# Where the MLP's pieces stand in ScalarE's order: top-k attention and a leaky-ReLU MLP on one core

## The chip, the cores and the metric

The kernel runs on one core of a Trainium2 chip. The metric is the device time of one execution in microseconds (us). The kernel before took 1473.86 us in the median of 4 runs (1472.53 to 1476.35). In what follows PE is TensorE (matmuls), DVE VectorE, ACT ScalarE, POOL GpSimd and SP the engine that issues the DMAs.

## What is computed

Attention with 8 batches, 8 heads, 576 positions and head dimension 64, in which each query keeps its 32 largest scores; its output, as 4608 rows of 512, goes through a two-layer MLP with a leaky ReLU. All is in 32-bit floats.

```python
scores = scale * np.matmul(q, k.transpose(0, 1, 3, 2))
kth = np.partition(scores, -32, axis=-1)[..., -32:-31]
scores = np.where(scores >= kth, scores, -1e9)
attn = np.exp(scores - scores.max(-1, keepdims=True))
attn = attn / (attn.sum(-1, keepdims=True) + 1e-9)
x = np.matmul(attn, v).transpose(0, 2, 1, 3).reshape(4608, 512)
h = x @ w_in                                  # 512 x 2048
out = np.maximum(0.01 * h, h) @ w_out         # 2048 x 512
```

## The kernel before

**Units.** The attention is cut into 144 units. A unit is 128 query rows against 576 keys for two heads: either 128 queries of one pair of heads, or the last 64 queries of two pairs. A unit passes through a pipeline over several steps of the main loop (lines 536 to 589), one unit entering per step, so that step s works on four generations at once:

- `scores` (line 203) of units s+2 and s+3, every second step: matmuls into PSUM tiles `wide` and `narrow`, and four ScalarE copies to `s_sb` (line 227). `wide` has two buffers, shared with the values and with the transposes on TensorE; `narrow` has one.
- `top_k` (line 243) of unit s on VectorE: two elementwise operations, four rounds of max and match-replace, in four slots (`slot()`).
- `mask` (line 262) of unit s-1 on GpSimd, then `exponents` (line 271) of its two heads on ScalarE, which leave sums in `z`, and `sums` (line 275), which gives `ze`.
- of unit s-2: `reciprocals` on VectorE (`rz`, line 281), `normalize` for two heads (line 284), then `transpose` (line 286): two ScalarE copies split the 32-bit words into 16-bit halves (line 293), each half is written to DRAM by a DMA on SP's queue (line 294), and a DMA transpose brings them back as `wT` (line 296). Four units near the start (14, 15, 23 and 31) are transposed on TensorE (line 306) and copied by ScalarE (line 312).
- `weigh_values` (line 326): matmuls of `wT` with the values, for two units at a time; `keep_values` (line 340) copies the result to `x`. For units up to 13 this happens early in a step (place MIDDLE), later at its end (END); line 447 says in which step: for an odd unit n from 14 on, n+3, or n+2 for three hurried ones.

**The MLP.** It works on chunks of tokens: two of 128 and 17 of 256. `mlp` (line 377) is a generator; between its `yield`s it issues a few matmuls, and each `yield` gives a cost in columns. First layer: `ph` (line 389; 512 columns for two matmuls of 256), and after each pair of feature blocks a Prelu on ScalarE (line 395) that empties the PSUM buffer. Second layer: `pz` (line 401; 1024 for two matmuls of 512), and after 16 feature blocks a ScalarE copy (line 410) and an output DMA on SP. The first two chunks are handled otherwise (line 351): `ph` with x as weights (line 357), Prelu (line 362), and transposes `pt` of the result on TensorE (line 373; cost 256) with a ScalarE copy (line 374). `ph`, `pz` and `pt` share one pool of two PSUM buffers.

**The planner.** `mlp_steps(budget)` (line 423) issues a piece: it adds the budget to an account and runs the generator until the account is used up; a cost that overdraws it is paid off by the next pieces, which may then issue nothing. There are 7 pieces per step. The budget is 500 as long as at most two chunks have become ready, later the backlog spread evenly over the pieces up to the next chunk (line 472).

**What sets the order.** Every engine works through its own instructions in the order in which the loop issues them. TensorE's order is that of MLP pieces, values, scores and the transposes on TensorE; ScalarE's is that of normalizations, exponents, splits, the copies and the Prelus of the pieces. A change of the loop's order changes both, and a wait in either holds up all that stands behind it on that engine.

In a step of the kernel before, ScalarE meets: normalization; pieces 1 and 2; exponents of the first head; both splits; pieces 3, 4 and 5; exponents of the second head and `sums`; copies of values and scores; pieces 6 and 7. In the first 20 steps the normalization mostly stands behind piece 1.

## Time and profile before

| | |
|---|---|
| median of 4 runs | 1473.86 us |
| the profiled execution | 1472.53 us |
| its span, first to last instruction | 1470.6 us |
| mean clock granted to TensorE | 0.98 |
| weights rounded, up to about | 64 us |
| first MLP matmul at | 132.9 us |
| last instruction of VectorE's top-k, about | 1384 us |
| DMA transpose, issue to landing (median of 140) | 4.5 us |

The span is a little shorter than the execution, and the profiled execution is the fastest of the four runs; sums made from the trace are sums within it. An engine's busy share is a mean over stages with different bounds. Busy time, the rows of a timeline (start in us, duration in us, engine, line, operation, output<-inputs, and in brackets the idle time before and what ended it) and the lists of waits are shown with the prediction.

### The profile page before, as it was taken

To read this page: it belongs to the slowest core of one execution; us is meant where nothing else is said; L and a number is where in the kernel's file an instruction comes from. 1 tells how busy PE (TensorE), PEld (TensorE's weight loads), DVE (VectorE), ACT (ScalarE), POOL (GpSimd) and SP (SyncE) were. 2 spreads that over 40 slices of the span, in tenths; PEclk is the share of its full clock that TensorE was granted. 3 is DMA by queue.
4 is the path that set the end of the run, shared out by engine and by line. 5 is a ranking of instruction groups with operands and counts; after the bars stand their busy time and mean duration, and the time that the engine had idled before them with its cause. 6 is when DMAs were issued, how large, how long until landed. Compare 5 with 4: busy or idle time off the path is not lost.

```text
span 1470.6 us, 24096 instructions
## 1 busy us (share of the span) xinstructions
PE 1395.5 (95%) x8068; PEld 928.5 (63%) x8068; DVE 1322.6 (90%) x3400; ACT 1095.8 (75%) x1979; POOL 1098.0 (75%) x743
## 2 busy tenths in 40 slices
PE   7716989999999999999999999999999999999999
PEld 2304547676766666666666666766676767676674
DVE  6999999999999999999999999999999999999600
ACT  8657877877787777777777777787877787877720
POOL 3288877888788888788888888888888888788700
PEclk9957999999999999999999999999999999999999
DMA  9725442654367554666557545565457555554510
GB/s 348 283 75 134 138 112 89 173 168 137 105 171 216 131 144 130 184 173 153 135 166 199 151 128 145 159 199 144 128 166 207 144 134 135 164 137 134 145 47 14
DMA packets 388795, 222.29 MB, mean 151 GB/s; under 512 B 333888, under 2 KB 333888, under 8 KB 386624
## 3 DMA queue, kind: packets, MB, share of 16 engines
q1 hardware_dynamic: 388672, 220.77, 52.9%
q8 instruction: 63, 1.03, 0.3%
q14 instruction: 60, 0.49, 0.1%
HBM read 46.14 MB, written 92.01 MB: 94 GB/s over the span
## 4 chain that ended last, share of the span: by engine, by line
PE 86%; DVE 11%; DMA 1%; issue 1%; ACT 1%; POOL 0%; DVEq 0%; ACTq 0%
PE pz L401 33%; PE ph L389 32%; PE wide L333 11%; PE wide L220 6%; DVE tops L255 4%; PE narrow L220 3%; DVE pairs L258 3%; DVE pairs L250 1%; DMA raw<-in_weights_dram 1%; DVE w_in L155 1%; DVE scale L152 1%; DMA wT<-apart 0%; DVE w_out L155 0%; DVE scale L129 0%; DVE top L138 0%
## 5 line engine op out<-in xcount | busy, mean ns | idle before, releaser
L268 POOL TENSOR_SCALAR pen<-s_sb,tops 128x576 f32<-128x576 f32 x288 | 638.3, 2216 | 208.0 <-DVE tops L255 119.0
L255 DVE MAX8 tops<-pairs 128x8 f32<-128x288 f32 (+1 forms) x1152 | 637.8, 594 | 0.0
L401 PE MATMUL pz<-w_out,gT 128*128 128x512 f32 x1152 | 510.7, 598 | 4.9 <-ACT scale L362 4.9
L389 PE MATMUL ph<-x,w_in 128*128 128x256 f32 x2176 | 481.1, 381 | 0.0
L258 DVE MATCH_REPLACE8 pairs<-tops,pairs 128x288 f32<-128x288 f32 (+1 forms) x864 | 461.5, 541 | 0.0
L389 PEld LDWEIGHTS ph<-x,w_in 128*128 128x128 f32 x2176 | 410.7, 190 | 77.1 <-issue 22.9
L269 POOL TENSOR_TENSOR s_sb<-s_sb,pen 128x576 f32<-128x576 f32 x288 | 407.4, 1415 | 24.0
L401 PEld LDWEIGHTS pz<-w_out,gT 128*128 128x128 f32 x1152 | 215.6, 190 | 269.7 <-issue 263.5
L293 ACT COPY split<-s_sb 128x1152 uint16<-128x1152 uint16 x280 | 307.1, 1146 | 0.0
L284 ACT ACTIVATE s_sb<-s_sb,rz 128x576 f32<-128x576 f32 x288 | 207.1, 769 | 42.3 <-DVE rz L281 42.3
L272 ACT ACTIVATE s_sb<-s_sb,nbias 128x576 f32<-128x576 f32 x288 | 221.4, 769 | 12.5 <-POOL s_sb L269 12.5
L250 DVE TENSOR_TENSOR pairs<-s_sb 128x576 f32<-128x576 f32 x288 | 213.6, 780 | 9.9
L333 PEld LDWEIGHTS wide<-wT,vt 128*64 128x64 f32 x3200 | 161.7, 139 | 65.7 <-ACT s_sb L227 27.2
L333 PE MATMUL wide<-wT,vt 128*64 128x128 f32 (+1 forms) x3200 | 178.8, 268 | 23.5 <-ACT s_sb L227 21.8
L395 ACT ACTIVATE gT<-ph 128x512 f32<-128x512 f32 x136 | 80.8, 594 | 80.0 <-PE ph L389 80.0
L347 ACT COPY x<-wide 128x128 f32<-128x128 f32 (+1 forms) x160 | 32.1, 260 | 127.6 <-PE wide L333 127.5
L227 ACT COPY s_sb<-wide 128x704 f32<-128x704 f32 x142 | 107.1, 754 | 25.4 <-PE wide L220 25.3
L220 PE MATMUL wide<-kt,qt 64*128 64x352 f32 (+1 forms) x392 | 75.7, 499 | 26.6 <-ACT s_sb L227 23.6
L227 ACT COPY s_sb<-narrow 128x448 f32<-128x448 f32 x142 | 68.7, 536 | 1.1 <-PE narrow L220 0.5
L410 ACT COPY o_sb<-pz 128x512 f32<-128x512 f32 x36 | 21.1, 585 | 59.2 <-PE pz L401 59.2
L258 DVE MATCH_VALUE_LOAD pairs<-tops,pairs 128x8 f32 x864 | 64.9, 75 | 0.0
L281 DVE RECIPROCAL rz<-ze 128x2 f32<-128x2 f32 x144 | 22.7, 157 | 45.7 <-ACT ze L277 45.5
(63 smaller groups left out, 622.8 us busy)
## 6 DMA issues: line engine op xcount, KB each, us to landing
apart<-split SPq DMA_DIRECT2D x280, 288.0 KB, 2.1
raw<-in_weights_dram SPq DMA_DIRECT2D x16, 1024.0 KB, 6.9
vt<-in_vk_dram SPq DMA_DIRECT2D x32, 320.0 KB, 3.4
out_dram<-o_sb SPq DMA_DIRECT2D x36, 256.0 KB, 2.0
qt<-in_qT_dram SPq DMA_DIRECT2D x20, 288.0 KB, 3.2
kt<-in_kT_dram SPq DMA_DIRECT2D x20, 288.0 KB, 3.6
raw<-in_qT_dram SPq DMA_DIRECT2D x12, 288.0 KB, 3.3
raw<-in_kT_dram SPq DMA_DIRECT2D x12, 288.0 KB, 3.6
```

Of the source, the lines that this page charges most:

```text
L220: nc.tensor.matmul(to[r0:r0 + u.rows, i, :], qt[d, u.q0:u.q0 + u.rows], kt[d, k0:k1], start=True, stop=True)
L250: nc.vector.tensor_tensor(pairs[:, :, n, :], u.both[:, :, 0:HS], u.both[:, :, HS:S], op)
L255: nc.vector.max(out=u.tops[:, i, r, :], in_=rest[i])
L258: nc.vector.match_replace(out=rest[i], in_to_replace=u.tops[:, i, r, :], in_values=rest[i], imm_value=LOWEST)
L268: nc.gpsimd.tensor_scalar(pen, u.s[i], u.tops[:, i, ROUNDS - 1, 7:8], MASKED, ALU.is_lt, ALU.mult)
L269: nc.gpsimd.tensor_tensor(u.s[i], u.s[i], pen, ALU.add)
L272: nc.scalar.activation(u.s[i], u.s[i], AF.Exp, bias=u.nbias[:, i:i + 1], scale=SCALE, accum_out=u.z[:, i:i + 1])
L284: nc.scalar.activation(u.s[i], u.s[i], AF.Copy, bias=0.0, scale=u.rz[:, i:i + 1])
L293: nc.scalar.copy(split, pairs[:, :, h])
L333: nc.tensor.matmul(po[side * D:(side + 1) * D, o, :], vt[:, c, side, :], u.wT[:, c + side * NKC if c + 1 < NKC else c, r:r + n], start=(c ...
L389: nc.tensor.matmul(ph[:, i, 0:n], w_in[c][:, f * P:(f + 1) * P], x[c][:, 0:n], start=(c == 0), stop=(c == HP - 1),)
L401: nc.tensor.matmul(pz[0:m, 0:DMODEL], gT[:, f, r0:r0 + m], w_out[f // 4][:, f % 4, :], start=(f == 0), stop=(f == NFC - 1),)
```

## The change

Three pieces change their place in a step. Piece 3 stands between the exponents of the first head and the splits. Piece 4 is handed to `transpose` as a function and issued after the first split and its DMA, ahead of the second split; where a unit is transposed on TensorE, or there is none, it follows at that place. Piece 6 stands behind the exponents of the second head and `sums`, ahead of the copies of values and of scores and of the values at the place END, and has the budget of step s; before, it stood behind them with the budget of step s+1. Pieces 1, 2, 5 and 7 and all else stay.

```diff
-    def transpose(u):
+    def transpose(u, between):
...
             nc.scalar.copy(split, pairs[:, :, h])
             nc.sync.dma_start(apart[:, h, :], split)
+            if h == 0:
+                between()
...
             if old:
                 exponents(old, 0)
+            mlp_steps(budget)
             if older:
-                keep_transposed(older) if s - 2 in HASTY else transpose(older)
+                keep_transposed(older) if s - 2 in HASTY else transpose(older, lambda: mlp_steps(budget))
+            if not older or s - 2 in HASTY:
+                mlp_steps(budget)
             slot()
-            mlp_steps(budget)
-            mlp_steps(budget)
             slot()
             mlp_steps(budget)
             if old:
                 exponents(old, 1)
                 sums(old)
+            mlp_steps(budget)
             if not at_once:
                 keep(weighed, s, MIDDLE)
...
             budget = slot_budget(s + 1)
-            mlp_steps(budget)
             mlp_steps(budget)
             load_more(s)
```

## The prediction

> **What bounds the kernel now.** I read, in this order: busy time by engine, busy time by stretch, TensorE's waits, and the timelines of TensorE and ScalarE around the one long wait that the change can reach.

> ```profile
> PE 1395.5 (95%) x8068; PEld 928.5 (63%) x8068; DVE 1322.6 (90%) x3400; ACT 1095.8 (75%) x1979; POOL 1098.0 (75%) x743
> ```

> TensorE is the busiest engine, and the stretches (busy us of TensorE first after the comma, its clock after POOL) say where its 75 us of idle time lie:

> ```profile
> 160.00:200.00 40.00, 35.27 (x182) 18.72 (x181) 39.69 (x103) 33.72 (x64) 33.29 (x24) 0.97 0.49 140
> 200.00:240.00 40.00, 38.93 (x285) 24.32 (x283) 36.58 (x98) 26.09 (x52) 31.87 (x22) 0.95 0.22 59
> 240.00:280.00 40.00, 40.00 (x312) 30.16 (x311) 37.87 (x102) 34.24 (x68) 32.45 (x22) 1.00 0.62 173
> ```

> From 240 us on, TensorE is busy in every microsecond but 0.62, at clock 1.00, and a stretch of 64 pz matmuls in the chain takes 27.48 us, 429 ns each, without slack. MLP's last chunk runs alone on it from 1411 us. So nothing after 240 us can be sped up by another order; the order can only make TensorE wait there. What can be won lies before 240 us, and the change touches only what lies behind the first MLP piece, at 132.9 us. TensorE's waits (us in total, times, longest):

> ```profile
> PE wide L333 <- ACT s_sb L227: 21.8, 2, 13.5
> ...
> PE pz L401 <- ACT scale L362: 4.9, 2, 4.2
> ...
> PE wide L333 <- ACT wT L312: 1.1, 1, 1.1
> PE wide L333 <- DMA wT<-apart: 0.6, 1, 0.6
> ```

> The first line lies before 132.9 us. The wait of 4.25 us is the one to look at: first TensorE, then ScalarE, in step 14.

> ```profile
> 193.53 0.60 PE L373 MATMUL pt<-ident,scale 128*128 128x128 f32 x4
> 198.37 3.78 PE L401 MATMUL pz<-w_out,gT 128*128 128x512 f32 x4 [4.25 <-ACT scale L362]
> 202.09 1.45 PE L220 MATMUL wide<-kt,qt 64*64 64x352 f32 x8
> ```
> ```profile
> 194.88 0.76 ACT L272 ACTIVATE s_sb<-s_sb,nbias 128x576 f32<-128x576 f32 x1
> 195.55 0.19 ACT L272 ACTIVATION_READ_ACCUMULATOR s_sb<-s_sb,nbias 128x1 f32 x1
> 195.64 2.19 ACT L293 COPY split<-s_sb 128x1152 uint16<-128x1152 uint16 x2
> 197.74 0.59 ACT L362 ACTIVATE scale<-ph 128x512 f32<-128x512 f32 x1
> ```

> pz needs the PSUM buffer that the Prelu of line 362 empties. Its input was finished at 193.5, but on ScalarE it stands behind the normalization (which waits for VectorE's rz until 193.53), the exponents and both splits.

> **Step 1: the Prelu comes ahead of the splits.** Which piece it is in follows from the planner: before piece 3 of step 14 the account stands at -88; 500 are added, so piece 3 issues the second half of ph (1024) with its Prelu; the account is then at -612, piece 4 issues nothing, and piece 5 (388) issues pt (256) and the first pz (1024). Piece 3 now precedes the splits. The Prelu starts at 195.64 and not at 197.74, and pz at about 196.25: **2.1 us**, the start-to-start time of the two splits. rz, due at 193.5, is not touched: VectorE is busy throughout up to there. In steps 7 to 13 I followed both engines in the same way: at most 0.6 us is gained (the 0.63 us wait at 154.19) and lost again at 190.0, where ph waits for a Prelu that stays behind both splits.

> **Step 2: the clock.** After the gap TensorE ran at half speed (clock: third number from the end):

> ```profile
> 196.00:198.00 2.00, 0.00 (x0) 0.00 (x0) 1.97 (x4) 2.00 (x3) 0.96 (x2) 0.88 0.17 67
> 198.00:200.00 2.00, 1.63 (x2) 0.84 (x3) 2.00 (x6) 1.76 (x5) 1.92 (x2) 0.50 0.64 236
> ...
> 204.00:206.00 2.00, 2.00 (x22) 1.01 (x15) 2.00 (x5) 1.51 (x4) 0.88 (x3) 0.91 0.01 2
> ```

> A mean of 0.88 and of 0.91 puts half speed between 197.5 and 204.4 us; the work from 198.37 to 204.4 took 6.0 us for 3.0. What a gap of 2.1 us does, no row shows exactly. Bounds: 0, if the clock still falls at 197.5 and stays down as long, and 3.0 us. The nearest wait is that of 2.35 us before 119.41: the four matmuls after it took 0.86 us, as at full clock (161.26). I take **3.0**. Against it: the clock did fall at about 122.4, after hardly 1 us of work; here unbroken work follows.

> [...]

> **Step 3: what the early stage gives back.** With 2.1 + 3.0 us, the values of units 10 and 11 start at 202.0 and not at 207.20. Next late is unit 14 in step 16. VectorE's wait for ze (2.09 us before 211.68) goes, since the score copies and the sums behind them follow TensorE, so rz comes at about 209.7; the two normalizations end at 211.1; TensorE, there at 210.0, waits about 0.9 us for them, and ends the transposes at 211.9 instead of 216.29: 4.4 us ahead. The values of units 14 and 15 (at 228.44 after 1.07 us of waiting) start at about 224.1. The early stage thus keeps **-4.3 us** (-1.8 at the low bound of step 2: of 8.2 us from 196.2 to 204.4, 6.8 would be at half speed, so 4.75 us of work are done there instead of 3.0). VectorE gains 2.09 and 1.09 us by the two waits and 1.85 us by a third (250.07), so it holds TensorE up nowhere later.

> **Step 4: the steady stage.** Nothing is added: the same splits, DMAs, Prelus and matmuls, reordered. Two moves matter: the second split now stands behind pieces 3 and 4, and values and scores come on TensorE behind piece 6. On SP, the transposes and a piece's output stay behind the same ScalarE work. The deadline is tight: a split's halves are written, then transposed (4.5 us to landing in the median, 4.2 to 6.3), and the values wait:

> ```profile
> 396.78 2.41 SPq L296 DMA_TRANSPOSE wT<-apart  x1
> ...
> 402.08 1.31 PE L333 MATMUL wide<-wT,vt 128*64 128x128 f32 x20 [0.62 <-DMA wT<-apart]
> ```

> From such rows I took the margin (landing of the odd unit's transpose to its first matmul) of all 64 groups of values after 240 us: 0.04 to 1.8 us in nearly all, median 1.17. From one group of scores to the next values TensorE has 14 pieces, before and after. In them the second split stood behind ScalarE's work of 4 pieces and stands behind that of 5. Score copies (0.9), normalizations (1.34), exponents (0.76) and splits (2.1) make 5.1 us; each Prelu or output copy ahead adds 0.49, and waits for its matmuls. Worked through step by step with the planner's account (matmuls 0.43 us per 256 columns), the split moves by -1.4 to +0.5 us (often earlier, since the normalization no longer queues behind a Prelu that waits for TensorE), the values by -1.72 to +1.72. Margins stay positive but for step 40 (its values come a piece of 1.72 us sooner: 1.16 becomes -0.56) and step 94 (0.14, with a landing of 6.11, becomes -0.35); step 36 (0.62 of waiting) stays near 0; late landings in the other margins below 0.4 may make 0.5. Together some 1.8 us of waits for 0.62: **+1.2 us**. Bounds: -0.6 (the one wait goes too) and +12.0 (every margin 1.0 smaller). PSUM is no new wait: a Prelu now comes sooner in ScalarE's order, and TensorE waited for none after 240 us.

> **Sum:** -4.3 + 1.2 = **-3.1 us**. The profiled execution took 1472.53 us (span 1470.6), so 1469.4 by it; it was the fastest of four, 1.33 us under their median of 1473.86, so 1470.8 as a median.

> **Rivals.**
> - *The clock falls all the same* (step 2 at 0): -1.8 + 1.2 = -0.6, 1473.3. For it: the fall at 122.4. Against: the full pace after 119.41.
> - *Nothing is given back*: margins hold, and unit 14 costs nothing: -5.2, 1468.7. For it: most margins grow in my working. Against: unit 14's chain runs through rz.
> - *Transposes come late* (slower): the second split, behind a Prelu that waits for TensorE, eats the margins of the values. A loss of 0.62 us in every margin makes waits of 4.3 us and cancels the gain; 1.0 us makes 12.0, so 1473.86 - 4.3 + 12.0 = 1481.6; 1.5 us makes 29. For it: ScalarE did wait for ph 53.9 us after 240 us, and the wait at 402.08 is this one. Against: the normalization gets ahead of such Prelus, and pieces between scores and values stay 14.
> - *The gap stays* (pz released by something else that is as late): only +1.2, 1475.1. Against it: pt's copy, the other input near, isn't needed by the first pz.

> **How the numbers follow.** Forecast 0.50 (1469.4 to 1472.2); nothing given back 0.16; clock falls 0.17; transposes late 0.13; gap stays 0.04. Less than 0.2% (2.9 us; about what can be told from no change) lies between 1470.9 and 1476.8. The forecast sits on that edge: half of it and all of the second case are faster, 0.41; the other half, the clock case and the gap case are within 0.2%, 0.46; late transposes are slower, 0.13. Range: from 1467.0 (below the second case by the medians' own scatter of 1.5) to 1476.0, which leaves out late transposes and the ends.

> **What would show it.** The Prelu between exponents and first split at 195.6; pz at 196.2; clock 1.00 through 197 to 204; values of 14 and 15 near 224; TensorE full after 240 with waits for wT under 2 us in total. Waits for wT above 4 us, or a clock of 0.50 after 197, prove me wrong at step 4 or 2.

## The result and the profile after

The changed kernel took 1471.05 us in the median of 33 runs (1468.68 to 1474.37), beside 1473.3 us (53 runs, 1471.0 to 1476.92) of the kernel before on the same chip. The ratio is 0.9983, with a 95% interval of 0.9979 to 0.9988: about 2.5 us faster. The forecast was 1470.8 us and 3.1 us faster; the range held the time.

In the changed kernel the line numbers move by two or three: values are L335, pz L403, ph L391 and its Prelu L397; of the first two chunks ph is L359, the Prelu L364, pt L375; the copy of wT is L314 and the DMA transpose L298. The split keeps L293.

The profiled execution has a span of 1468.7 us (before: 1470.6). First the busy time of TensorE, from the page:

```profile
PE 1393.6 (95%) x8068; PEld 927.8 (63%) x8068; DVE 1322.1 (90%) x3400; ACT 1098.1 (75%) x1979; POOL 1097.7 (75%) x743
```

The same number of matmuls takes 1.9 us less of busy time. TensorE's waits (us in total, times, longest):

```profile
PE pz L403 <- ACT scale L364: 2.4, 2, 2.1
...
PE wide L335 <- DMA wT<-apart: 1.1, 2, 0.6
PE ph L391 <- ACT gT L397: 0.8, 1, 0.8
```

pz waits 2.14 us where it waited 4.25; transposes are waited for a little more; and the last line is new. TensorE's rows around the gap (start, duration, in brackets the wait):

```profile
194.19 0.60 PE L375 MATMUL pt<-ident,scale 128*128 128x128 f32 x4
196.93 1.98 PE L403 MATMUL pz<-w_out,gT 128*128 128x512 f32 x4 [2.14 <-ACT scale L364]
```

And ScalarE's, in the same stretch:

```profile
195.54 0.76 ACT L272 ACTIVATE s_sb<-s_sb,nbias 128x576 f32<-128x576 f32 x1
...
196.30 0.57 ACT L364 ACTIVATE scale<-ph 128x512 f32<-128x512 f32 x1
196.78 2.19 ACT L293 COPY split<-s_sb 128x1152 uint16<-128x1152 uint16 x2
```

The Prelu now stands between the exponents and the splits, and pz starts 0.63 us after it. The same four pz matmuls take 1.98 us where they took 3.78. The stretches of 2 us show why (the clock is the third number from the end):

```profile
196.00:198.00 2.00, 1.07 (x3) 0.59 (x4) 2.00 (x5) 2.00 (x5) 0.89 (x3) 1.00 0.03 8
198.00:200.00 2.00, 2.00 (x23) 0.89 (x25) 1.97 (x4) 2.00 (x3) 2.00 (x1) 1.00 0.47 177
...
204.00:206.00 2.00, 2.00 (x26) 1.51 (x23) 2.00 (x6) 2.00 (x4) 1.55 (x2) 1.00 0.66 148
```

The clock reads 1.00 throughout, where it was 0.88, 0.50 and 0.91.

**Where the time went.** I set each matmul of the changed kernel beside the same matmul of the kernel before and took the difference of their starts, each counted from the start of its own span. A falling number is a gain, a rising one a loss.

| near (us, in the kernel before) | after minus before (us) | what lies in between |
|---|---|---|
| 133.4 | +1.16 | ahead of the change: a start 0.6 us later, and half clock up to 134.53 us (before: 132.68) |
| 190.0 | +0.66 | waits at 154.19 and 189.50 us shrink or go, 1.1 gained; ph waits 0.43 us at 190.65, 0.6 given back |
| 205.3 | -4.34 | gap and clock: **5.0 gained** |
| 230.8 | -4.04 | units 14 and 15: 0.3 given back |
| 424.9 | -4.52 | the wait of 0.62 us at 402.08 is gone; 0.5 lost ahead of it, in no wait |
| 468.7 | -2.70 | steps 40 to 44: **1.8 given back** |
| 1066.7 | -1.98 | a wait for a transpose, 0.43 us |
| end | -1.88 | |

From 190 us on the changed kernel gains 2.54 us, and from 133.4 us on 3.04. The 1.16 us that it is behind at 133.4 us belong to this execution and not to the change. The losses between 425 and 469 us have two rows with a wait in them:

```profile
432.80 1.31 PE L335 MATMUL wide<-wT,vt 128*64 128x128 f32 x20 [0.62 <-DMA wT<-apart]
466.03 1.99 PE L391 MATMUL ph<-x,w_in 128*128 128x256 f32 x8 [0.81 <-ACT gT L397]
```

The first is step 40, where the prediction had a wait of 0.56 us. The second is a PSUM buffer behind a Prelu, which the prediction had excluded. By the starts of the matmuls behind them the two cost 0.78 and 0.99 us: in these traces a wait costs some 0.2 us more than its row shows.

### The profile page after: what moved, and what is told of

It reads as the page before. It is cut to its first block, busy times and chain, and to the rows that moved or that the text cites. A ratio compares the mean times of both kernels' runs of the same rounds, so it can differ in the third digit from the quotient of the medians.

```text
span 1468.7 us, 24096 instructions
## 1 busy us (share of the span) xinstructions
PE 1393.6 (95%) x8068; PEld 927.8 (63%) x8068; DVE 1322.1 (90%) x3400; ACT 1098.1 (75%) x1979; POOL 1097.7 (75%) x743
## 3 DMA queue, kind: packets, MB, share of 16 engines
q8 instruction: 63, 1.03, 0.3%
## 4 chain that ended last, share of the span: by engine, by line
PE 83%; DVE 11%; DMA 3%; ACT 2%; issue 1%; POOL 0%; DVEq 0%; SPq 0%; ACTq 0%
PE pz L403 32%; PE ph L391 32%; PE wide L335 10%; PE wide L220 6%; DVE tops L255 5%; DVE pairs L258 4%; PE narrow L220 3%; DMA raw<-in_weights_dram 2%; DVE pairs L250 1%; DMA wT<-apart 1%; ACT s_sb L284 0%; DVE scale L152 0%; DVE w_out L155 0%; ACT s_sb L227 0%; ACT wT L127 0%
## 5 line engine op out<-in xcount | busy, mean ns | idle before, releaser
L403 PE MATMUL pz<-w_out,gT 128*128 128x512 f32 x1152 | 504.7, 594 | 2.4 <-ACT scale L364 2.4
L391 PE MATMUL ph<-x,w_in 128*128 128x256 f32 x2176 | 482.9, 381 | 0.8 <-ACT gT L397 0.8
L391 PEld LDWEIGHTS ph<-x,w_in 128*128 128x128 f32 x2176 | 409.4, 190 | 77.6 <-issue 22.2
L403 PEld LDWEIGHTS pz<-w_out,gT 128*128 128x128 f32 x1152 | 216.4, 190 | 267.2 <-issue 262.8
L293 ACT COPY split<-s_sb 128x1152 uint16<-128x1152 uint16 x280 | 309.5, 1147 | 0.0
L272 ACT ACTIVATE s_sb<-s_sb,nbias 128x576 f32<-128x576 f32 x288 | 222.4, 772 | 13.8 <-POOL s_sb L269 13.8
L335 PEld LDWEIGHTS wide<-wT,vt 128*64 128x64 f32 x3200 | 161.7, 139 | 66.0 <-issue 34.7
L335 PE MATMUL wide<-wT,vt 128*64 128x128 f32 (+1 forms) x3200 | 179.1, 269 | 24.4 <-ACT s_sb L227 22.2
L227 ACT COPY s_sb<-wide 128x704 f32<-128x704 f32 x142 | 107.1, 754 | 20.9 <-PE wide L220 20.9
L397 ACT ACTIVATE gT<-ph 128x512 f32<-128x512 f32 x136 | 80.6, 593 | 54.1 <-PE ph L391 53.3
L220 PE MATMUL wide<-kt,qt 64*128 64x352 f32 (+1 forms) x392 | 75.1, 493 | 26.0 <-ACT s_sb L227 23.6
L227 ACT COPY s_sb<-narrow 128x448 f32<-128x448 f32 x142 | 68.7, 536 | 0.6
```

Source lines behind the costliest of these rows:

```text
L220: nc.tensor.matmul(to[r0:r0 + u.rows, i, :], qt[d, u.q0:u.q0 + u.rows], kt[d, k0:k1], start=True, stop=True)
L272: nc.scalar.activation(u.s[i], u.s[i], AF.Exp, bias=u.nbias[:, i:i + 1], scale=SCALE, accum_out=u.z[:, i:i + 1])
L293: nc.scalar.copy(split, pairs[:, :, h])
L335: nc.tensor.matmul(po[side * D:(side + 1) * D, o, :], vt[:, c, side, :], u.wT[:, c + side * NKC if c + 1 < NKC else c, r:r + n], start=(c ...
L391: nc.tensor.matmul(ph[:, i, 0:n], w_in[c][:, f * P:(f + 1) * P], x[c][:, 0:n], start=(c == 0), stop=(c == HP - 1),)
L403: nc.tensor.matmul(pz[0:m, 0:DMODEL], gT[:, f, r0:r0 + m], w_out[f // 4][:, f % 4, :], start=(f == 0), stop=(f == NFC - 1),)
```

## The experiments

Ratios are to the kernel before, run in turn with each kernel on the same chip (its median was 1473.3 us for the first row, and 1474.46 to 1475.02 us for the others). Each kernel was profiled once.

| kernel | median us | ratio, 95% interval |
|---|---|---|
| the changed kernel | 1471.05 | 0.9983, 0.9979 to 0.9988 |
| only_step14 | 1471.04 | 0.9978, 0.9969 to 0.9987 |
| all_but_step14 | 1475.87 | 1.0009, 1.0 to 1.0018 |
| piece3_alone | 1474.46 | 1.0002, 0.9993 to 1.001 |
| piece4_alone | 1474.82 | 1.0001, 0.9992 to 1.001 |
| piece6_alone | 1474.56 | 1.0, 0.9991 to 1.0009 |
| gap_filled | 1472.85 | 0.9991, 0.9982 to 0.9999 |
| step14_and_6 | 1470.89 | 0.9973, 0.9964 to 0.9982 |
| prelu_before_norm | **1469.12** | 0.996, 0.9948 to 0.9973 |
| after_capped | 1474.39 | 0.9999, 0.9991 to 1.0008 |
| best_capped | 1470.29 | 0.9972, 0.9962 to 0.9982 |
| before_capped | 1475.33 | 1.001, 1.0002 to 1.0019 |
| best_light_vector | 1468.44 | 0.9957, 0.9943 to 0.9971 |

The last one leaves out a part of the top-k search, so it is a probe and no rival to the others.

**Which step holds the gain.** For five kernels I made each of the three moves depend on a condition; with all three true in every step it is the changed kernel, with all false the kernel before.

```diff
+            p3, p4, p6 = (s == 14,) * 3        # only_step14
+            p3, p4, p6 = (s != 14,) * 3        # all_but_step14
...
             if old:
                 exponents(old, 0)
-            mlp_steps(budget)
+            if p3:
+                mlp_steps(budget)
...
+            if not p3:
+                mlp_steps(budget)
```

> The kernel before, with the three pieces moved in step 14 alone. Theory A (the whole gain is the Prelu of step 14 that gets ahead of the splits, with the clock that then stays up; elsewhere the change costs about 1.3 us of new waits): pz of step 14 starts 2.1 us sooner, the clock stays at 1.00 through 197 to 205 us, the one wait for wT near 400 us stays, and the time is 3 to 4.3 us below the kernel before, about 1469.6 us, at or below the changed kernel. Theory B (the pieces spread over every step are what pays, step 14 is one of many): at most 1 us below the kernel before, about 1472.5 us.

> The three pieces moved in every step but step 14. Theory A: the gap of 4.25 us before pz in step 14 and the half clock behind it are back, the steady stage has about 1.9 us of waits instead of 0.6, so 0 to 1.5 us above the kernel before, about 1474.3 us. Theory B: nearly the whole gain of the change stays, 2 to 2.5 us below the kernel before, about 1471 us.

The three moves in the one step 14 give the whole gain (ratio 0.9978), and the moves in all other steps give none (1.0009). In the profile of only_step14 the gap is 1.67 us and the clock 1.00; 5.0 us are gained between 190 and 216 us, and 2.8 us of them are lost later, with waits for wT at 396.70, 448.62 and 467.99 us and one of 0.52 us for the load of v at 598.54. In all_but_step14 the gap is 4.25 us and the clock halves. Outside step 14, then, the change is worth nothing to the time.

**Each piece alone.** The same conditions, in every step:

```diff
+            p3, p4, p6 = True, False, False    # piece3_alone
+            p3, p4, p6 = False, True, False    # piece4_alone
+            p3, p4, p6 = False, False, True    # piece6_alone
```

> Piece 3 alone moved ahead of the splits, in every step; pieces 4 and 6 as before. Theory A: the gap of step 14 closes to about 2.1 us as in the changed kernel, values and scores keep their old places, so 2.5 to 4.3 us below the kernel before, about 1470 us. Theory B (the even spread needs all three): about a third of the gain, 0.8 us below, about 1472.5 us.

> Piece 4 alone moved, between the two splits, in every step. Theory D (a gain comes only from a Prelu that gets ahead of the splits in step 14, where piece 4 is empty; elsewhere the time follows from the margins between the landing of a transpose and the values, which the second split behind piece 4 makes smaller): gap of 4.2 us and half clock as before, median margin about 1.0 us instead of 1.17, 0 to 1 us above the kernel before. Theory B (each piece that is spread pays for itself): 0.8 us below the kernel before.

> Piece 6 alone moved, ahead of the copies, values and scores, in every step. Theory D: gap of 4.2 us and half clock as before; values come one piece later against an unmoved second split, so the median margin grows to about 2.3 us; waits for wT in total under 1 us; the time within 0.7 us of the kernel before, since there was only 0.6 us of such waits to remove. Theory B: 0.8 us or more below the kernel before.

piece3_alone missed the number expected of it. The early gain is there: the gap is 2.14 us, the clock stays at 1.00, and TensorE is about 4 us ahead at 230 us. But all of it, 5.8 us, is lost again between 450 and 1380 us, at the first matmuls of a dozen groups of values. The rows of their waits hold 3.2 us (2.5 for wT, 0.7 for the load of v), and each wait costs some 0.2 us more than its row: the group with a row of 0.29 us at 449.72 starts 0.47 us later, and the one with 0.74 at 469.15 starts 0.91 later. The margin, by which the odd unit's transpose lands ahead of the first matmul that needs it, explains it. Over the 64 groups of values after 240 us:

| kernel | median margin (us) | groups below 0.5 us |
|---|---|---|
| before | 1.17 | 10 |
| piece3_alone | 0.80 | 25 |
| piece4_alone | 1.00 | 18 |
| piece6_alone | 2.52 | 4 |
| the changed kernel | 2.03 | 6 |

A piece ahead of a split makes the split wait behind its Prelu, in every step; piece 6, moved ahead of the values on TensorE, gives the transpose a piece more of time. So pieces 3 and 6 are read as a pair: the first wins 5 us in step 14 and would lose them again, the second wins nothing itself and pays for the first. No run has these two without piece 4. Piece 4 does neither: in piece4_alone the gap is 3.19 us (4.2 had been expected), the clock halves, and nothing is left.

**The clock by itself.** gap_filled is the kernel before, order and all, with the four transposes pt ahead of the gap issued nine times over, so that TensorE works through most of the gap.

```diff
-                yield from turned(j - 1, g_of)
+                yield from turned(j - 1, g_of, 9 if (ch, j) == (1, 3) else 1)
...
-        for i in range(4):
+        for i in [n % 4 for n in range(4 * times)]:
```

> The kernel before with its order unchanged; the four transposes of pt in step 14, just ahead of the gap of 4.25 us, are issued nine times over (the same result written again), which fills about 4 us of the gap with TensorE work and moves pz by nothing, or by up to 0.3 us. Theory A's second term (half the gain is the clock): clock 1.00 through 197 to 205 us, pz and the scores behind it at full pace, 3.0 us saved there, less up to 0.9 us that unit 14's normalization gives back; about 1470.8 us, 2 to 3 us below the kernel before. Theory C (the clock would have cost nothing in the end, only the earlier pz counts): as the kernel before, within 0.5 us of 1473.3 us.

The Prelu is as late as before, and still TensorE goes from 0.31 us late at 190 us to 2.69 us ahead at 205 us: 3.0 us, at clock 1.00. That is the prediction's price of the clock in this one execution, shown without its step 1. Of the whole time only 1.3 us are left (0.9991), less than the 2 to 3 us expected: in this kernel's order the margins are the narrow ones of before, and a wait of 1.37 us for wT follows at 254.09.

**More of the same in step 14.** step14_and_6 has pieces 3 and 4 moved in step 14 only, and piece 6 in every step. prelu_before_norm has in addition pieces 2 and 3 ahead of the normalization in step 14.

```diff
+            p3, p4, p6 = s == 14, s == 14, True     # step14_and_6, prelu_before_norm
+            if p3:                                  # prelu_before_norm only
+                mlp_steps(budget)
+                mlp_steps(budget)
             if older and late:
                 weights_of(older)
-            if s - 2 in HASTY:
+            if s - 2 in HASTY and s != 16:
                 transpose_in_haste(older)
-            mlp_steps(budget)
+            if not p3:
+                mlp_steps(budget)
+            if s == 16:
+                transpose_in_haste(older)
```

> All three pieces moved in step 14, and piece 6 in every step; pieces 3 and 4 elsewhere as before. Theory D: the early stage gains the 5 us of the changed kernel, and with margins of about 2.3 us in the median the steady stage keeps them: 4 to 5 us below the kernel before, 1 to 2 us below the changed kernel. Theory E (whatever the early stage gains, about 2 us of it are given back in the steady stage because TensorE then runs ahead of VectorE between 390 and 560 us, where VectorE is at full pace): 3 us below the kernel before, as with step 14 alone.

> As the kernel with step 14 and piece 6, and besides: in step 14 pieces 2 and 3 stand ahead of the normalization, so that the Prelu no longer queues behind the wait for rz, and in step 16 piece 2 stands ahead of the transposes on TensorE. Theory D: the rest of the gap in step 14, 2.1 us, goes too, TensorE has 1.7 us of matmuls to do while unit 14 is normalized, and 1.5 to 2 us more are kept: 6 us below the kernel before. Theory F (units 14 and 15, whose chain runs through VectorE, now set the early stage): the 2.1 us come back as a wait for them in steps 16 and 17, and the time is that of the kernel with step 14 and piece 6 within 0.5 us.

step14_and_6 came out at the edge of what was expected: 4.0 us faster, with margins of 2.53 us in the median. Its interval (2.7 to 5.3 us) holds Theory E's 3 us too, and its trace gives back 3.8 us between 425 and 514 us, so the two theories aren't told apart by the time. In prelu_before_norm the Prelu no longer waits for rz, and the gap all but goes. Its rows on TensorE, then on ScalarE:

```profile
194.31 1.98 PE L403 MATMUL pz<-w_out,gT 128*128 128x512 f32 x4 [0.25 <-ACT scale L364]
```
```profile
193.66 0.60 ACT L364 ACTIVATE scale<-ph 128x512 f32<-128x512 f32 x1 [1.99 <-PE ph L359]
194.15 1.43 ACT L284 ACTIVATE s_sb<-s_sb,rz 128x576 f32<-128x576 f32 x2
```

The normalization pays 0.6 us for it (194.15 us, where rz had let it start at 193.5 in the kernel before), and nobody waits for that. TensorE is 6.96 us ahead at 205 us. It is the best kernel of the study, 5.9 us faster than before, and beats the changed kernel too. But it also loses 3.4 us between 425 and 514 us.

**Why the lead is lost there.** In steps 34 to 42 the planner's share is 439 to 524 columns a piece, against 585 in most later steps, so TensorE's steps are short: two of them, from one group of values to the next, take 16.7 us in the kernel before, against 18.5 later. The first idea was to spread the shares: hold back MLP work before step 34 for these steps.

```diff
-        return backlog[0] / ((until + 1 - s) * SLOTS)
+        most = 543 if s < 34 else 1e9
+        return min(backlog[0] / ((until + 1 - s) * SLOTS), most)
```

> The changed kernel with the planner's share held to at most 543 columns a piece in the steps before 34, where it runs at 549 to 585; what is held back is MLP work that fills steps 34 to 41, which then hold 585 columns a piece in place of 439 to 527. No matmul is added or left out. Theory G (the gain of step 14 is given back between 425 and 470 us because TensorE's steps are too short there, so it catches up with VectorE's chain and waits for the second half's transpose): the waits at 433 and 466 us fall below 0.3 us together and the give-back of 1.8 us between 425 and 469 us with them; the whole kernel gains 1 to 2 us on the changed kernel, a ratio to the kernel before of 0.9965 to 0.998, 1469 to 1470 us beside a before of 1473.5. Rival H (those waits are set by the DMAs that run beside the transposes, and come wherever loads are dense): waits stay where the loads are, no gain, within 0.5 us of the changed kernel. Rival I: the work held back makes TensorE wait earlier, in steps 20 to 33, for the same chain of VectorE; waits of 1 us and over between 240 and 370 us and no gain.

> The kernel of prelu_before_norm with the share held to at most 543 columns a piece before step 34. Its give-back between 425 and 514 us was 3.4 us (waits of 1.03, 1.01 and 0.79 us). Theory G: 1.5 to 3 us of it are kept, a ratio of 0.994 to 0.995 to the kernel before, 1465 to 1467 us beside 1473.5. Rival H: waits stay, 1468 to 1469. Rival I: 1468 to 1470 with waits before 370 us.

> The kernel before with the share held to at most 543 columns a piece before step 34. In the kernel before TensorE comes 4.5 us later to these steps and waits there 0.62 us for one transpose only. Theory G: nothing much to win, 0 to -0.7 us, a ratio of 0.9995 to 1. Rival H: 0. Should it gain over 1.5 us, the cap helps by something else than the give-back of step 14's gain, and what after_capped gains is no evidence for G.

It was wrong. The cap makes each of the three kernels slower, by 1.5 to 2.4 us if the ratios are compared (for the best one the intervals overlap). In after_capped and best_capped the waits at 430 and 450 us go, and others come in the steps that were made shorter, as Rival I had it. In best_capped, on TensorE:

```profile
243.46 6.31 PE L391 MATMUL ph<-x,w_in 128*128 128x256 f32 x28 [1.86 <-ACT gT L397]
...
322.97 1.31 PE L335 MATMUL wide<-wT,vt 128*64 128x128 f32 x20 [1.01 <-DMA wT<-apart]
```

after_capped waits 1.64 us at 325.24, before_capped 1.22 us at 324.63. So the shares decide where TensorE waits, not whether. The shorter steps are not the whole of it: in after_capped the transpose of step 28 lands 8.74 us after its second split, and in the changed kernel, where nothing waits there, 6.90 us.

The last kernel asks whose pace the transpose follows. VectorE works 39.7 of 40 us between 400 and 440 us, so its search was made lighter in the steps ahead of the waits.

```diff
-            if r + 1 < ROUNDS:
+            if r + 1 < ROUNDS and not (light and r == 1):
...
-            picks = top_k(cur) if cur else iter(())
+            picks = top_k(cur, 32 <= s < 44) if cur else iter(())
```

> The kernel of prelu_before_norm with the two MATCH_REPLACE8 of the second round of the top-k search left out in steps 32 to 43, so that the search of these units takes out the wrong scores (that part of the computation is changed); every other instruction stays. VectorE saves 0.85 us a step there (two loads of 0.07 and two replacements of 0.44 us, less their overlap), 10 us in 12 steps; no transfer, no matmul and no ScalarE work changes. Theory J (the gain of step 14 is given back where TensorE overtakes VectorE, which works 39.6 to 39.7 of 40 us there, and so comes late with the mask, the normalization and the transpose): the waits at 431, 449 and 469 us (2.8 us in all) fall below 0.3 us each, TensorE's lead on the kernel before stays at 5 to 6 us at 514 us where it was 3.0, and the time is 1465.5 to 1467 us beside 1473.5 of before, a ratio of 0.994 to 0.995. Rival H (the transposes land late because transfers run beside them, 4.6 to 6.4 us, whenever they are issued): the waits stay above 0.5 us each and the ratio is 0.996, as without this edit.

Neither theory has it whole. VectorE is no longer full (37.7 of 40 us between 400 and 440), and ScalarE's wait for rz before the normalization, 1.71 us at 426.50 in prelu_before_norm, is 0.23. The three waits of TensorE shrink from 1.03, 1.01 and 0.79 us to 0.45, 0.30 and 0.44, so Rival H, which had them above 0.5 us, missed; but they don't go below 0.3 us, and the time is that of prelu_before_norm within the intervals. Over three rounds of values (415.14 to 468.71 us, and 417.54 to 469.48) TensorE takes 53.57 us against 51.94; less the waits, 50.74 against 50.75. So the lighter search took 1.64 of the 2.83 us, and 1.19 us are left.

It did not do so in Theory J's way, by an earlier normalization and split. The waits end with the odd unit's transpose, and the second split of that unit ends as long after the group of values before it in both kernels: 8.65, 8.70 and 10.18 us. What became shorter is the way from there to the landing: 7.38, 9.17 and 9.26 us became 6.80, 8.46 and 8.91, which is 1.64 us together. That is the place where Rival H looks; how VectorE's work bears on those transfers isn't shown. What TensorE waits for in step 40 shows in the rows of best_light_vector on ScalarE, and on SP's queue:

```profile
418.85 0.43 ACT L349 COPY x<-wide 128x128 f32<-128x128 f32 x2 [2.97 <-PE wide L335]
...
421.25 0.77 ACT L227 COPY s_sb<-wide 128x704 f32<-128x704 f32 x1
421.89 1.46 ACT L284 ACTIVATE s_sb<-s_sb,rz 128x576 f32<-128x576 f32 x2
...
423.99 2.20 ACT L293 COPY split<-s_sb 128x1152 uint16<-128x1152 uint16 x2
```
```profile
428.35 2.40 SPq L298 DMA_TRANSPOSE wT<-apart  x1
```

This is a loop. The values end on TensorE; ScalarE, which waited for them, copies them and the scores that follow them (418.85 to 422 us), normalizes the next unit, takes exponents and splits (to 426.2); the halves are written, the transpose is issued at 428.35 and lands 4.65 us later, at 433.00; and at 433.13 TensorE starts the matmuls that need it, having waited 0.45 us. After its first row ScalarE has no idle time of over 0.4 us in it, and from the values to the second split's end the four rounds ahead of steps 38 to 44 took 8.65 us or more in each of the 14 kernels. This round of the loop takes 15.6 us (417.54 to 433.13), and TensorE's own work in it is 15.1. The loop is read off these rows; no run was made to shorten it.

That it is only 15.1 us comes from piece 6. The times from one group's later matmuls to the next group's, each with the wait that it ends in:

| kernel | to step 38 | to step 40 | to step 42 | to step 44 | lost from 425 to 514 us |
|---|---|---|---|---|---|
| before | 17.66 | 16.69 | 16.69 | 18.57 | |
| the changed kernel (both, with pieces 3 and 4) | 18.46 | 15.76 (0.62) | 16.74 | 19.55 | 1.8 |
| all_but_step14 (the same, no lead) | 18.51 | 15.80 (0.65) | 18.00 (1.09) | 18.53 | 2.1 |
| only_step14 (lead, piece 6 as before) | 17.66 | 16.69 | 17.56 (0.71) | 19.37 (0.67) | 1.6 |
| piece6_alone (no lead) | 18.52 | 15.93 (0.79) | 18.01 (1.10) | 18.86 (0.17) | 2.6 |
| step14_and_6 (both) | 18.47 | 16.04 (0.90) | 18.68 (1.77) | 19.28 (0.58) | 3.8 |
| prelu_before_norm (both) | 18.47 | 16.17 (1.03) | 17.92 (1.01) | 19.49 (0.79) | 3.4 |
| best_light_vector (both, VectorE lighter) | 18.47 | 15.59 (0.45) | 17.21 (0.30) | 19.14 (0.44) | 1.8 |

And what each group waits for, as the time from the group before it to the end of the odd unit's second split, plus the time from there to the landing of its transpose:

| kernel | step 40 | step 42 | step 44 |
|---|---|---|---|
| before | 8.65 + 6.88 | 9.08 + 7.26 | 10.23 + 7.48 |
| the changed kernel | 8.65 + 6.97 | 8.95 + 7.57 | 10.61 + 7.65 |
| all_but_step14 | 8.66 + 7.00 | 8.87 + 9.09 | 10.66 + 7.01 |
| only_step14 | 8.65 + 7.08 | 9.12 + 8.40 | 10.18 + 9.14 |
| piece6_alone | 8.65 + 7.14 | 8.71 + 9.26 | 10.18 + 8.64 |
| prelu_before_norm | 8.65 + 7.38 | 8.70 + 9.17 | 10.18 + 9.26 |

Two things, then, make the loss. Wherever piece 6 is moved, the two steps ahead of the values of step 40 hold 1.7 us of MLP less, and those ahead of step 38 0.8 us more; TensorE's 15.1 us there are shorter than the loop, with a lead and without. At steps 42 and 44 TensorE's own work, 16.7 to 16.9 and 18.5 to 18.7 us, is longer than 8.7 to 9.1, or 10.2 to 10.7, us with the 7 us that the transfers take elsewhere. Outside the capped kernels it waits there only where they take 8.2 us or more. In only_step14 the splits come no later behind the values than in the kernel before, so its lead did not run into VectorE's chain: the transfers took 1.1 and 1.7 us longer. all_but_step14 has such late transfers at step 42 with no lead at all, and the changed kernel, with a lead, has none. At step 42 it is the writes of the halves that are late, at step 44 mostly the transpose; what makes them late in one kernel and not in another stays open. The losses don't add up: 1.6 and 2.6 us alone, 3.4 and 3.8 together.

## Why the prediction was right, and where it was not

- **Step 1, the Prelu ahead of the splits: right.** The gap went from 4.25 to 2.14 us, 2.11 us for a predicted 2.1. It was piece 3 in step 14, as the planner's account had said; only_step14 and piece3_alone both have this gain. In the steps ahead of it 1.1 us were gained and 0.6 given back; at most 0.6, and all of it back, had been set down.
- **Step 2, the clock: right in the profiled execution, and wrong as a constant.** Of 5.0 us between 190 and 205 us 2.1 are the gap's, so 2.9 are the clock's, and gap_filled shows 3.0 alone. But the clock's gain hangs on more than the length of the gap, and the rival in which it falls all the same came true in one execution of this order: in after_capped, which issues the same as the changed kernel up to step 17, the gap is again 2.14 us and the clock does halve, from 198.09 to 201.51 us (rows in the last section). TensorE is busy for all of these 3.42 us, so an estimate of the cost is half of them, 1.7 us of the 3.0.
- **Step 3, what the early stage gives back: right in kind, a little too dear.** 4.7 us were kept at 230.8 us for a predicted 4.3; the values of units 14 and 15 started at 224.40 (predicted 224.1) after the same wait of 1.07 us. Unit 14's chain gave back 0.3 us where 0.8 had been set down (5.1 to 4.3).
- **Step 4, the steady stage: the mechanism was right and its size too small.** +1.2 us was the forecast, +2.16 the measurement (from -4.04 us at 230.8 to -1.88 at the end). Step 40 waited 0.62 us for a predicted 0.56, for the reason given: its values come a piece sooner. Step 36 did not wait, as predicted; step 94, the other one named, did not wait either (a margin of 0.82 us). Two things were missing from the sum. "PSUM is no new wait": there was one, 0.81 us at 466.03, for a buffer that a Prelu empties. And step 108 waited 0.43 us for a transpose that took 6.23 us to land, where the kernel before had 4.55: late landings were put at 0.5 us in all, in margins that were narrow already, and this margin had been 0.75. With what a wait costs beyond its row, steps 40 and 108 and the PSUM wait cost 0.78, 0.61 and 0.99 us. That VectorE "holds TensorE up nowhere later" is not refuted: the splits of steps 40 to 44 come no later behind the values with a lead than without. The changed kernel's 1.8 us between 425 and 469 us don't need the lead, as all_but_step14 loses 2.1 us between 425 and 514 us without it.
- **The rival "transposes come late"** is not what happened, but it is what piece 3 alone does: the margins fell to 0.80 us and the whole gain was lost. The prediction had the counterweight (values and scores behind piece 6) in its working and not in its list of rivals.
- **Right by more than its own merit.** 1470.8 against 1471.05 is nearer than the terms are: the loss was 1.0 us larger, the keep 0.4 better, and the clock, by the estimate below, is worth less than 3.0 us in the mean. The kernel before, too, came out at 1473.3 us and not at the 1473.86 that the sum starts from, which made up for a gain of 2.5 us where 3.1 had been forecast. An estimate from the profiled executions, with half of TensorE's busy time at clock 0.50 as the cost: a gap of 3.7 to 4.25 us cost 3.0 us in the kernel before and 1.7 each in all_but_step14, piece6_alone and before_capped, 2.0 in the mean; one of 2.14 us cost 1.7 in after_capped and nothing in the changed kernel and piece3_alone, 0.6 in the mean. By that the difference is worth some 1.5 us and not 3.0. How often the clock falls in either kernel was not measured, as each was profiled once.

## What to carry to other kernels

Look for the one instruction that frees what the bounding engine waits for, and put it ahead of independent work in its own engine's order in that one place: here the gain of the whole change lay in one step of 148, and the same reordering everywhere else was worth nothing by itself. For every later deadline count the work between one use and the next against the shortest round of the loop that feeds it, and expect a lead that the bounding engine wins early to be lost at the first steps in which that loop, or a late transfer in it, is the longer. Price a gap and the clock drop behind it apart: here the clock halved behind all five gaps of 3.19 to 4.25 us, behind one of three of 2.14 us, and behind none of the six of 1.7 us and less. Shortening the gap to 2.14 us won its 2.1 us in each of the three executions and the clock in two; all but closing it (0.25 us in prelu_before_norm) won both.

## What the runs showed of the hardware

```profile
194.12:197.54 3.42, 0.01 (x1) 0.00 (x0) 3.42 (x8) 3.42 (x6) 2.21 (x4) 1.00 0.33 74
197.54:200.95 3.41, 2.58 (x3) 1.17 (x4) 3.38 (x10) 2.23 (x6) 3.23 (x3) 0.50 0.48 178
```

then of after_capped:

```profile
194.68:198.09 3.41, 1.27 (x7) 0.70 (x6) 3.41 (x8) 3.31 (x6) 2.48 (x3) 1.00 0.68 146
198.09:201.51 3.42, 3.42 (x12) 1.06 (x14) 3.38 (x9) 2.92 (x6) 3.06 (x2) 0.50 0.47 177
```

and of piece3_alone:

```profile
195.19:198.60 3.41, 1.78 (x4) 0.68 (x4) 3.38 (x8) 3.41 (x6) 2.29 (x3) 1.00 0.39 86
198.60:202.02 3.42, 3.42 (x36) 1.80 (x36) 3.42 (x12) 3.39 (x9) 3.24 (x3) 1.00 0.46 173
```

after_capped and piece3_alone have the same gap of 2.14 us. In the first it lies inside one stretch, which is 37% busy, and the clock is 0.50 in the next; in the second it is shared by two stretches, 85% and 52% busy, and the clock stays at 1.00. In the changed kernel the two shares were 65% and 72%, and it stayed too. At this place a stretch of 0 to 37% was followed by half clock in six executions; in the other eight none was under 52%, and the clock stayed. From 0.50 it came back to 1.00 after stretches that were 84% busy (piece4_alone) and 100% (the other five); the one of 76% in the kernel before was followed by a second at 0.50. At 112 to 123 us, where the work is values and scores, stretches of 38 to 49% were followed by half clock in seven executions, and one of 42% (115.62 to 119.03 us in the kernel before) was not; what tells them apart isn't shown. So the same order up to step 17 had half clock in one execution (after_capped) and none in another (the changed kernel), and one profile doesn't give the price of a drop.

**The write ahead of a transpose took longer with more in flight; the transpose itself scattered.** From issue to landing a transpose took 4.5 to 4.6 us in the median of every kernel, up to 6.3 in the changed one and 6.97 us in piece3_alone. After 240 us the median was about the same whether or not another transfer of SP's queue was in flight meanwhile (4.52 and 4.58 us in the kernel before, 4.55 and 4.62 in the changed one), so what makes the late ones isn't shown. The write of a unit's first half did differ with that, after 240 us in the 14 executions: 2.1 us in the median with no transpose and no load in flight at its issue (735 cases), as with loads alone (147); 2.2 with a transpose and no load (567); 3.8 with a transpose and one load (100), and 4.0 with a transpose and two or more loads (201). The late ones meet the narrow margins in some steps and not in others, and losses in the steady stage come as single waits, of up to 1.86 us in these traces (best_capped, at 243.46).
